# Retention followed by an ELU feed-forward layer: two-level Strassen products replaced by three products of 12-bit float32 parts

## The chip, the cores and the metric

The kernel runs on one core of a Trainium2 chip. The core has a matrix engine (PE; its weight loads are listed apart as PEld), three engines for elementwise work (DVE, ACT, POOL), and a queue (SP) that issues every data transfer (DMA) of this kernel. The metric is the time of one execution in microseconds (us); the median of several executions is given. All times below come from the three timed runs and from one profiled execution of the kernel before.

## The reference

Three steps are computed in float32: a recurrent attention (retention) over 4 batches of 8 heads, 768 tokens and 64 dimensions; then a feed-forward layer from 512 to 2048 features with an ELU; then one from 2048 back to 512.

```python
for t in range(S):                                   # S = 768, H = 8, D = 64
    state = gamma[None, :, None, None] * state + np.einsum('bhd,bhe->bhde', k[:, :, t], v[:, :, t])
    y[:, :, t] = scale * np.einsum('bhd,bhde->bhe', q[:, :, t], state)
x = np.ascontiguousarray(attn_out.transpose(0, 2, 1, 3)).reshape(B * S, H * D)   # 3072 x 512
h = x @ w_in                                         # 512 -> 2048
g = np.where(h > 0.0, h, alpha * (np.exp(np.minimum(h, 0.0)) - 1.0))
return (g @ w_out).astype(np.float32)                # 2048 -> 512
```

## The kernel before

**Blocks.** The 3072 tokens are cut into six blocks of 512. Each block needs its retention first (`scores`, `states`, `outputs`: many float32 products of 64x64), then layer 1 (`w_in`, 16 groups of 128 features, 4 products of 128x128 weights by 512 tokens each) and layer 2 (`w_out`, 4 output groups, 16 products each). Written plainly, one layer of one block is 64 products of a 128x128 weight tile by 512 tokens.

**Opening.** Weights arrive as 64-bit numbers. SP loads sixteen pieces of 1 MB (L149), ACT turns each into float32 parts in three passes (`prepare`, L171, L173, L175), and DVE joins them (`decode`, L198 and L201). Beside that, PE computes the retention of block 0 and its layer 1 by plain float32 products (`plain_first`, L518 and L542), and the scores and states of block 1.

**Strassen.** Everything after that is Strassen's scheme in Winograd's form, which needs 7 half-size products for 8. Layer 2 of block 0 (`second_of_first`, L632) and layer 1 of block 1 (`first`, L765) use one level. Layer 2 of block 1 (`second_twice`, L924) uses two levels. Blocks 2 and 3, and then 4 and 5, are taken together, 1024 tokens at a time: layer 1 uses two levels for four of the seven products (`big_twice`, L1152) and one level for the other three (`big_rest`, L1199), and layer 2 uses two levels throughout (`second_big`, L1248). DVE makes the sums and differences of operands (L894, L1230) and of products (L1260, L1208), ACT moves products out of PE's accumulators (L1163, L1256) and computes the two steps of the ELU (L1214, L1215), which DVE ends (L1216).

**Weights.** Sums of weight blocks are formed once on DVE, written to a scratch area in memory, and read back for every later block in pieces of 128x512 numbers, 256 KB each (`want`, `fetch`, L830), in a fixed order, into a ring of buffers; a buffer is asked for again when PE has done with it.

**Order.** The scheduling is manual: each engine executes its instructions in the order in which the program text issues them. Lists such as `ORDER1`, `BIG2` and `VISITS` say where the retention of the next block goes between the products. POOL has little to do: it multiplies the values of a 128-token chunk by their powers of gamma (`scale_v`, L293), 16 times.

Of the kernel before, what the change touches and what calls it, by code (L numbers as in the profile page):

```python
# [10 lines left out]
FP32 = mybir.dt.float32  # L11
I32 = mybir.dt.int32
# [3 lines left out]
ALU = mybir.AluOpType  # L16


@with_exitstack
def kernel(  # L20
# [4 lines left out]
    scratch: bass.AP,  # L25
    scratch2: bass.AP,
    scratch3: bass.AP,
    scratch4: bass.AP,
# [3 lines left out]

# [6 lines left out]
    C = P  # L60
# [7 lines left out]
    NQ = 4  # L68
    NF = DFF // P // 2
# [7 lines left out]
    epool = ctx.enter_context(tc.tile_pool(name="epool", bufs=2))  # L77
    mid = ctx.enter_context(ExitStack())
    mpool = mid.enter_context(tc.tile_pool(name="mpool", bufs=4))
    hpool = mid.enter_context(tc.tile_pool(name="hpool", bufs=4))  # L80
    small = mid.enter_context(tc.tile_pool(name="small", bufs=6))
# [3 lines left out]

    early = ctx.enter_context(ExitStack())
    stage = early.enter_context(tc.tile_pool(name="stage", bufs=3, side="right"))
    t4 = early.enter_context(tc.tile_pool(name="t4", bufs=1, side="right"))
    so_ = t4.tile([P, 2, 7, 256], FP32, name="so")


    gnames = ["C11", "C12", "C21", "C22", "T3"]
    gq = {x: const.tile([P, DFF // P // 2, TH], FP32, name="g" + x) for x in gnames}
    gq["T1"] = gq["C12"]
    four = lambda x: gq[x].rearrange("p (i a) t -> p i (a t)", a=2)
    g_plain = [four(x)[:, i, :] for x in gnames[:4] for i in range(4)]

# [4 lines left out]
    def load(m, cuts=(0, 2048), behind=None):  # L102

        if m >= NCHUNK:
            return
        t = ldpool.tile([P, 2048], FP32, name="chunk", tag="chunk")
        raw[m] = (
            t[:, 0:1024].rearrange("p (a h c) -> p a h c", a=2, c=C),
            t[:, 1024:2048].rearrange("p (a h d) -> p a h d", a=2, d=D),
        )  # L110
        hold(t, behind)
        for lo, hi in itertools.pairwise(cuts):
            nc.sync.dma_start(t[:, lo:hi], qkv[m, :, lo:hi])

    def hold(t, other):

        if other is not None:
            nc.gpsimd.tensor_copy(t[0:1, 0:1], other[0:1, 0:1])

    w_all = const.tile([P, NQ, 14 * TH], FP32, name="w_all")
    w_a_, w_b_, w_x_ = (
        w_all[:, :, 1024 * g : 1024 * g + 1024].rearrange("p n (f c k d) -> p n f c k d", f=2, c=2, k=2) for g in range(3)
    )
    w_y_ = w_all[:, :, 3072:3584].rearrange("p n (f k d) -> p n f k d", f=2, k=2)
    w_a, w_b, w_x, w_y = ([x[:, n] for n in range(NQ)] for x in (w_a_, w_b_, w_x_, w_y_))
    s_of = lambda n: (w_y[n], w_x[n][:, :, 0], w_x[n][:, :, 1])
    NPIECE = 2 * NQ + NF  # L130
# [20 lines left out]

    def prepare(parts=1, by_vector=False, between=None):

# [4 lines left out]
        if n < 2 * NQ:  # L160
            dst = (w_a, w_b)[n % 2][n // 2].rearrange("p a b c d -> p (a b c d)")
        else:

            dst = w_x[n % NQ].rearrange("p a b c d -> p (a b c d)")
        todo = []
        for part in range(parts):
# [3 lines left out]
            lo, hi, flat = t[:, c, 0], t[:, c, 1], dst.bitcast(U32)[:, c]  # L170
            nc.scalar.activation(flat, lo, AF.Copy, scale=2.0**-29)  # L171
            top = dst.bitcast(F8).rearrange("p (c b) -> p c b", b=4)[:, c, 3]
            nc.scalar.activation(top, hi.bitcast(FP32), AF.Copy, scale=2.0**-120, saturate=False)  # L173
            if not by_vector:
                nc.scalar.activation(lo.bitcast(FP32), hi.bitcast(FP32), AF.Copy, scale=2.0**-112)  # L175
            todo.append((lo, flat, hi if by_vector else None))
        prepared.append((dst, todo))


    ORDER_F = [f for n in range(NF // 2) for f in (n, NF // 2 + n)]  # L180


    quarters = lambda f: scratch.rearrange("(s k) p (f c) -> k f p s c", k=2, f=4)[f // 4, f % 4]

    used = lambda f, a, b: slice(a, b, 2 if f < NF // 2 else 1)

    def decode(fine=False):

# [4 lines left out]
        decoded.append(dst.rearrange("p (a b) -> p a b", a=2))  # L193
        vec = nc.vector
        for c, flat, hi in todo:
            if hi is not None:
                vec.tensor_scalar(c.bitcast(FP32), hi.bitcast(FP32), 2.0**-112, None, ALU.mult)
# [3 lines left out]
            vec.tensor_tensor(out=flat, in0=c, in1=flat, op=ALU.add)  # L201
            yield
        load_piece()
        if n >= 2 * NQ:
            f = ORDER_F[n - 2 * NQ]
            nc.sync.dma_start(quarters(f)[:, used(f, 2, 8)], dst.rearrange("p (s c) -> p s c", c=P)[:, used(f, 2, 8)])
# [4 lines left out]

    blank = hpool.tile([P, TB], FP32, name="blank", tag="h")
    nc.vector.memset(blank, 0.0)

# [9 lines left out]
    begin = so_.rearrange("p n s c -> p (n s c)")  # L226
# [10 lines left out]
    nc.vector.tensor_scalar(vf, vf, scale, None, ALU.mult)  # L237

    causal = begin[:, 2 * S : 2 * S + P]
# [4 lines left out]
    identity = begin[:, 2 * S + P : 2 * S + 2 * P]  # L244
# [9 lines left out]
    post = begin[:, S : 2 * S]  # L254
# [20 lines left out]


    xb = const.tile([P, 4, TB], FP32, name="xb")
    xt_ = const.tile([P, 4, 2, TH], FP32, name="xt")
    xt = [xt_[:, n] for n in range(4)]

    x_of = lambda tb: xb if tb in (0, 3, 5) else xt_.rearrange("p j a t -> p j (a t)")

    xt1 = [xb[:, n].rearrange("p (a t) -> p a t", a=2) for n in (1, 2, 3, 0)]
# [15 lines left out]
    def state(tb, n):  # L299
# [3 lines left out]
        if (tb, n) == (0, 3):  # L303

            return xt[0].rearrange("p a t -> p (a t)")[:, 0:256].rearrange("p (h e) -> p h e", e=D)
# [79 lines left out]
    def outputs(tb, pp):  # L385
# [18 lines left out]
        for sub in range(2):  # L404
            nc.vector.tensor_tensor(
                out=place_of(x_of(tb)[:, :, 2 * pp * C : 2 * (pp + 1) * C])[:, :, :, sub, :], in0=y[sub],
# [67 lines left out]
    def combine_x_parts(tb=None):  # L474
        sub = lambda o, x, y: nc.vector.tensor_tensor(out=o, in0=x, in1=y, op=ALU.subtract)
        b11, b12, b21, b22 = (x_of(tb)[:, 2 * r : 2 * r + 2, half[t]] for r in range(2) for t in range(2))
        t1, t2, t3, t4_ = xt1 if tb == 1 else xt
        sub(t1, b12, b11)
        yield
        sub(t2, b22, t1)  # L480
        yield
        sub(t3, b22, b12)
        yield
        sub(t4_, b21, t2)

# [7 lines left out]
    def elu(g, h, depth=1, then=None):  # L493


        r = epool.tile([P, 512], FP32, name="r", tag="r", bufs=3)
        e = r if len(h.shape) == 2 else r.rearrange("p (a c) -> p a c", c=P)
        nc.scalar.activation(e, h, AF.Relu, scale=-1.0)
        nc.scalar.activation(e, e, AF.Exp, scale=-1.0)

        def last():
            nc.vector.scalar_tensor_tensor(g, e, -1.0, h, ALU.add, ALU.max)
            if then:
                then()

        while len(later) >= depth:
            later.pop(0)()
        later.append(last)

    def plain_first():  # L510

        tiles = [(n, w, row, fi) for n in range(NQ) for w, row in ((w_a, 0), (w_b, 1)) for fi in range(2)]
        banks = []

        def part(k, columns):
            n, w, row, fi = tiles[k]
            for j in range(4):
                nc.tensor.matmul(  # L518
                    banks[k][:, columns], lhsT=w[n][:, fi, j // 2, j % 2, :], rhs=xb[:, j, columns],
                    start=(j == 0), stop=(j == 3), skip_group_check=True,  # L520
                )

        for k in range(5):
            hp = bank("aabd"[k]) if k < 4 else ps_r.tile([P, 2, TH], FP32, name="hp", tag="r")
            banks.append(hp.rearrange("p a b -> p (a b)"))
# [8 lines left out]
        for k in range(5):  # L534
            part(k, half[1])
            n, w, row, fi = tiles[k]
            elu(g_plain[row * NF + 2 * n + fi], banks[k])
            yield
        for k, (n, w, row, fi) in enumerate(tiles[5:]):
            hp = bank("aabd"[k % 4]).rearrange("p a b -> p (a b)")  # L540
            for j in range(4):
                nc.tensor.matmul(  # L542
                    hp, lhsT=w[n][:, fi, j // 2, j % 2, :], rhs=xb[:, j, :], start=(j == 0), stop=(j == 3)
                )
            elu(g_plain[row * NF + 2 * n + fi], hp)
# [3 lines left out]
    def of_first(r, f, t, count=2):  # L549

        i = (r * NF + f) % 4
        g = gq[gnames[(r * NF + f) // 4]]
        return g[:, 2 * i + t] if count == 1 else g[:, 2 * i + t : 2 * i + 4 : 2, :]

    inputs = {}

    def inputs_of_first(f, slots):

        b11, b12, b21, b22 = (of_first(r, f, t) for r in range(2) for t in range(2))
        t3, t2, t4_ = slots  # L560
        tt = lambda o, x, y: nc.vector.tensor_tensor(out=o, in0=x, in1=y, op=ALU.subtract)
        tt(t3, b22, b12)
        tt(b12, b12, b11)
        yield
        tt(t2, b22, b12)
        tt(t4_, b21, t2)
        for x in range(2):
            inputs[f + x] = {
                1: of_first(0, f + x, 0, 1), 2: of_first(1, f + x, 0, 1), 3: of_first(1, f + x, 1, 1),
                4: t4_[:, x], 5: of_first(0, f + x, 1, 1), 6: t2[:, x], 7: t3[:, x],  # L570
            }
        yield

    sums = {}

    def sums_of_pieces(n):

        odd = n // 2 % 2
        t = so_[:, :, 3:7] if odd else so_[:, :, 0:4]
        both = w_all[:, n % NQ : n % NQ + 2, 2048:3072]  # L580
        a21, a11, a12, a22 = (both[:, :, 256 * d : 256 * d + 256] for d in range(4))
# [1307 lines left out]
```

## Time and profile before

| what | value |
|---|---|
| median of 3 runs | 621.36 us (620.31 to 621.38) |
| span of the profiled execution | 621.4 us |
| PE busy | 611.4 us (98%), 5446 records |
| DVE busy | 496.7 us (80%), 776 instructions |
| ACT busy | 261.0 us (42%) |
| POOL busy | 21.2 us (3%) |
| moved by DMA | 125.14 MB, mean 201 GB/s |
| granted clock of PE | 1.00 in every stretch |

The profiled execution's span is within 0.1 us of the median, so its rows can be added up against the measured time directly. A float32 product appears as two matmul records, each with its own weight load. "Mean ns of one" is how long one instruction takes from start to end; matmuls follow each other faster than that, since the next starts while the one before drains, so the pace of PE has to be read from runs of many records.

### The profile page before, as it was taken

The page shows a single profiled execution, that of the slowest core. Times are in us where ns is not written, and L with a number is a line of the kernel's source. Part 1 is how long each engine was busy: PE and PEld are TensorE (multiplying, and loading weights), DVE is VectorE, ACT ScalarE, POOL GpSimd, SP SyncE. Part 2 cuts the span into 40 slices and gives each one's busy share as a digit, 9 for nine tenths or more (in the row PEclk, how much of TensorE's full clock was granted, in tenths as well). Part 3 has the DMA queues.
Part 4 walks back from the last instruction along what each step waited for, and adds up shares of the span by engine and source line. Part 5 has one row for each costly group of instructions (what it writes and reads, how often), then busy time and mean ns, then how long its engine had stood idle before and what let it go on. Part 6 is the DMA issues. An engine that isn't in the chain of part 4 may idle for free.

```text
span 621.4 us, 13415 instructions
## 1 busy us (share of the span) xinstructions
PE 611.4 (98%) x5446; PEld 480.9 (77%) x5446; DVE 496.7 (80%) x776; ACT 261.0 (42%) x446; POOL 21.2 (3%) x30
## 2 busy tenths in 40 slices
PE   8999999999999999999999999999999999999998
PEld 6764568888889998888545888888888744788886
DVE  5768889989889875677888987898546897888885
ACT  5888844205542111236898210100144798511110
POOL 2011000000000001000010000110000000000000
PEclk9999999999999999999999999999999999999999
DMA  8697569789575898786811445873654523356453
GB/s 295 285 374 303 174 205 269 235 242 274 204 234 151 301 374 310 231 250 199 274 49 67 122 134 154 268 275 108 206 159 143 151 69 93 118 148 187 153 150 117
DMA packets 79278, 125.14 MB, mean 201 GB/s; under 512 B 6128, under 2 KB 46832, under 8 KB 74480
## 3 DMA queue, kind: packets, MB, share of 16 engines
q1 hardware_dynamic: 79216, 124.28, 62.1%
q8 instruction: 43, 0.70, 0.4%
q14 instruction: 19, 0.16, 0.1%
HBM read 94.63 MB, written 29.62 MB: 200 GB/s over the span
## 4 chain that ended last, share of the span: by engine, by line
PE 86%; DVE 4%; DMA 3%; ACT 3%; issue 2%; SPq 0%; DVEq 0%
PE pa L1248 15%; PE pa L1152 9%; PE pd L1248 8%; PE pa L1199 6%; PE pd L1152 4%; PE pa L765 4%; PE pd L1199 4%; PE pb L1248 4%; PE x L632 3%; DMA wq<-scratch_dram 2%; PE pa L924 2%; PE pa L542 2%; PE pb L1152 2%; PE pa L632 2%; PE pb L1199 2%; PE y L415 2%
## 5 line engine op out<-in xcount | busy, mean ns | idle before, releaser
L1256 ACT COPY ms<-pa 128x256 f32<-128x256 f32 x41 | 15.3, 372 | 108.5 <-PE pa L1248 105.5
L1248 PE MATMUL pa<-gC,wq 128*128 128x256 f32 x224 | 53.1, 381 | 0.0
L1248 PEld LDWEIGHTS pa<-gC,wq 128*128 128x128 f32 x224 | 42.1, 190 | 6.8 <-DVE gT L1216 0.5
L1215 ACT ACTIVATE r<-r 128x512 f32<-128x512 f32 x64 | 40.3, 630 | 2.0
L1163 ACT COPY m<-pa 128x512 f32<-128x512 f32 x32 | 18.7, 585 | 48.9 <-PE pa L1152 48.8
L293 POOL TENSOR_TENSOR chunk<-chunk,vf 128x512 f32<-128x512 f32 x16 | 18.0, 1124 | 381.3 <-DMA chunk<-in_qkv_dram 201.1
L1260 DVE TENSOR_TENSOR res<-pd,ms 128x256 f32<-128x256 f32 x26 | 11.0, 422 | 25.0 <-PE pd L1248 14.1
L1152 PE MATMUL pa<-ts,wq 128*128 128x256 f32 x104 | 26.9, 384 | 0.0
L1248 PE MATMUL pa<-ts,wq 128*128 128x256 f32 x112 | 26.8, 382 | 0.0
L1248 PE MATMUL pd<-w_all,wq 128*128 128x256 f32 x112 | 26.6, 380 | 0.1
L171 ACT ACTIVATE w_all<-wraw 128x1024 uint32<-128x1024 uint32 (+1 forms) x19 | 19.2, 1008 | 16.9 <-PE x L632 9.0
L1248 PE MATMUL pd<-ts,wq 128*128 128x256 f32 x104 | 24.7, 380 | 0.2 <-DVE ts L894 0.2
L1230 DVE TENSOR_TENSOR gC<-w_all,gC 128x1024 f32<-128x1024 f32 x20 | 24.2, 1260 | 0.0
L1248 PEld LDWEIGHTS pd<-w_all,wq 128*128 128x128 f32 x112 | 21.2, 190 | 3.4 <-DVE w_all L894 0.6
L1248 PEld LDWEIGHTS pa<-ts,wq 128*128 128x128 f32 x112 | 21.0, 190 | 2.9
L1248 PE MATMUL pa<-w_all,wq 128*128 128x256 f32 x96 | 22.9, 381 | 0.0
L173 ACT ACTIVATE w_all<-wraw 128x1024 fp8e4<-128x1024 f32 (+1 forms) x19 | 22.6, 1189 | 0.6
L1152 PEld LDWEIGHTS pa<-ts,wq 128*128 128x128 f32 x104 | 19.3, 190 | 4.5 <-ACT m L1163 0.8
L1216 DVE SCALAR_TENSOR_TENSOR w_all<-r,w_all 128x512 f32<-128x512 f32 x32 | 22.0, 688 | 0.7 <-ACT r L1215 0.6
L1248 PEld LDWEIGHTS pd<-ts,wq 128*128 128x128 f32 x104 | 19.7, 190 | 3.2 <-DVE ts L894 0.6
L1199 PE MATMUL pa<-ts,wq 128*128 128x512 f32 x48 | 22.1, 592 | 0.0
L1199 PE MATMUL pa<-gC,w_all 128*128 128x512 f32 x48 | 22.1, 592 | 0.0
(327 smaller groups left out, 1458.0 us busy)
## 6 DMA issues: line engine op xcount, KB each, us to landing
wq<-scratch_dram SPq DMA_DIRECT2D x191, 256.0 KB, 3.2
chunk<-in_qkv_dram SPq DMA_DIRECT2D x22, 1024.0 KB, 7.6
wraw<-in_w_dram SPq DMA_DIRECT2D x15, 1024.0 KB, 7.1
out_dram<-res SPq DMA_DIRECT2D x7, 512.0 KB, 3.3
scratch_dram<-gT SPq DMA_DIRECT2D x12, 256.0 KB, 4.3
wq<-scratch_dram SPq DMA_DIRECT2D x24, 128.0 KB, 3.1
scratch_dram<-w_all SPq DMA_DIRECT2D x12, 256.0 KB, 3.4
scratch_dram<-w_all SPq DMA_DIRECT2D x24, 128.0 KB, 3.2
```

The source lines that it names most:

```text
L171: nc.scalar.activation(flat, lo, AF.Copy, scale=2.0**-29)
L173: nc.scalar.activation(top, hi.bitcast(FP32), AF.Copy, scale=2.0**-120, saturate=False)
L293: eng.tensor_tensor(out=v, in0=v, in1=vf[:, i].unsqueeze(2).to_broadcast([C, H, D]), op=ALU.mult)
L632: nc.tensor.matmul(X[j][:, d, :], lhsT=w[j][:, d * P : d * P + P], rhs=x[j], start=(n == 0 and d == 0), stop=at_end, skip_group_check=True,)
L765: nc.tensor.matmul(ps[:, fi, :], lhsT=w[:, fi, j2, :], rhs=x[:, j2, :], start=(begin and fi == 0 and j2 == 0), stop=(j2 == 1), skip_group_ ...
L1152: nc.tensor.matmul(ps[:, f, :], lhsT=w[:, f, :], rhs=big_xs[j][k], start=(begin and f == 0), stop=True, skip_group_check=True,)
L1163: nc.scalar.copy(o, ps)
L1199: nc.tensor.matmul(ps, lhsT=w[:, k, :], rhs=layer_x[j][:, k], start=False, stop=(k == 1), skip_group_check=True,)
L1215: nc.scalar.activation(r, r, AF.Exp, scale=-1.0)
L1216: return lambda: nc.vector.scalar_tensor_tensor(g, r, -1.0, g, ALU.add, ALU.max)
L1230: nc.vector.tensor_tensor(out=quarter(to, r, t), in0=quarter(x, r, t), in1=quarter(y, r, t), op=op)
L1248: nc.tensor.matmul(ps, lhsT=w[:, f, :], rhs=ts[j][k][:, f // 2, f % 2, :], start=(begin and f == 0), stop=(f == 3), skip_group_check=True,)
```

## The change

All Strassen code goes, together with its sums, its four scratch areas and its ring (some 1,000 lines). Layer 1 of block 0 stays as it was. Every other layer becomes three products of parts, in the type float32r:

- Each operand is cut into a high part of 12 bits (`hi`), the rest (`lo`), and a third part `d` that is made from the two. The product is the sum of `hi` by `hi` and `lo` by `lo`, scaled in the accumulator by 1 + 2^-12 (`scaled`), plus the product of the two `d`.
- Weights of layer 1 are cut in block 1 (`parts_of_w_in`: one instruction on ACT, one on DVE, two transfers of 256 KB to scratch); `d` of them is made by POOL, for every 128 features in every block (`third_of_w_in`). Weights of layer 2 are cut in block 0 (`parts_of_w_out`: one on ACT, two on DVE over 128x1024, two transfers of 512 KB). From block 2 on, each 128x512 part is read back from scratch: `hi` and `lo` of `w_in`, `lo` and `d` of `w_out`; `hi` of `w_out` stays in place.
- Activations are cut in every block: `split_g` per 128 features (ACT, DVE, and DVE again, or POOL in block 0), and `split_x` (two halves: ACT, DVE, DVE).
- Each of the five blocks 1 to 5 is now computed alone, layer 1 and then layer 2. Retention of the next block goes between groups of layer 1 (`visit`, at groups 4, 6, 8, 10, 12).

Lines that begin with + in the core of the diff:

```diff
+    def parts_of_w_out(m):
+        src, hi = decoded[NPW + m], flat(wo1[:, 2 * m : 2 * m + 2])
+        lo = wpool.tile([P, 1024], F32R, name="p2", tag="p2", bufs=3)
+        d = wpool.tile([P, 1024], F32R, name="p3", tag="p3", bufs=1)
+        nc.scalar.activation(hi, src, AF.Copy, scale=PART * CUT)
+        stt(lo, src, PART, hi, ALU.subtract)
+        stt(d, hi, R, lo, ALU.subtract)
...
+    def split_g(f, by_pool=False):
...
+        nc.scalar.activation(g_hi[f], g[f], AF.Copy, scale=R * CUT)
+        stt(g_lo[f], g_hi[f], -1.0 / R, g[f], ALU.add)
+        (nc.gpsimd if by_pool else nc.vector).tensor_tensor(out=g_d[f], in0=g_lo[f], in1=g_hi[f], op=ALU.subtract)
...
+    def third_of_w_in(tb, f):
+        if f < NF:
+            got[tb, 4, f] = ring.tile([P, TB], F32R, name="w3", tag="w3", bufs=3)
+            nc.gpsimd.tensor_tensor(out=got[tb, 4, f], in0=got[tb, 1, f], in1=got[tb, 0, f], op=ALU.subtract)
...
+    def one_pass(ps, w, x, start=False, stop=False):
+        nc.tensor.matmul(ps, lhsT=w, rhs=x, start=start, stop=stop, skip_group_check=True)
...
+    def first(tb, f):
+        hp = flat(ps_r.tile([P, 2, TH], FP32, name="hp", tag="r") if f < 2 else bank("aabd"[(f - 2) % 4]))
+        for n in range(2):
+            for k in range(NK):
+                one_pass(hp, got[tb, n, f][:, k * P : k * P + P], xp[:, n, k], start=(n == 0 and k == 0))
+        scaled(hp, tb == 1 and f % 2 == 1)
+        yield
+        for k in range(NK):
+            one_pass(hp, got[tb, 4, f][:, k * P : k * P + P], xp[:, 2, k], stop=(k == NK - 1))
+        elu(f, hp)
...
+    def second_layer(tb, acc, between=None, beside=lambda f: None):
+        for f in range(3):
+            second(tb, acc, f, (0, 1))
+        if between:
+            between()
+            flush()
+        for f in range(NF):
+            second(tb, acc, f, (2, 3) if f < 3 else range(4))
+            if tb:
+                fetch()
+            if f + 3 < NF:
+                split_g(f + 3, tb == 0)
+            beside(f)
...
+    second_layer(0, acc, None, beside_first)
+    mid.close()
+    ring = ctx.enter_context(tc.tile_pool(name="ring", bufs=8))
+    want_out(0)
+    fetch(8)
```

In layer 2, `second` issues the first two products of a group for its output groups, and `end_of_second` issues the third products of all 16 groups after the accumulators have been scaled. In block 0, `beside_first` puts `parts_of_w_out` and the decoding of the next weight piece beside groups 1, 3, 5, 7 and 9 of layer 2; the other three pieces are cut during layer 1 of block 0.

## The prediction

> **What bounds the kernel now.** I read the busy shares first, then the chain that ended last, then the chain in order of time, and then single groups by shape.
>
> ```profile
> PE 611.4 (98%) x5446; PEld 480.9 (77%) x5446; DVE 496.7 (80%) x776; ACT 261.0 (42%) x446; POOL 21.2 (3%) x30
> ...
> PE 86%; DVE 4%; DMA 3%; ACT 3%; issue 2%; SPq 0%; DVEq 0%
> ```
>
> PE works nearly without a break and carries 86% of the chain. DVE is 80% busy, but its work lies beside PE's. So a change pays by the PE time it removes, less the waits of PE that it adds. The pace of PE stands in the chain in order of time:
>
> ```profile
> 86.57 2.59 PE x L632 x12
> ...
> 297.49 1.72 PE pa L1199 x4
> ...
> 348.67 2.02 PE sc L319 x128
> ...
> 362.97 2.01 PE kv L359 x110
> 364.99 1.93 PE pa L1248 x8
> 366.91 1.73 PE pb L1248 x8
> ```
>
> Eight records of 256 columns take 1.73 us, 0.216 each; four of 512 take 1.72, 0.430 each. A float32 product has two records, so 128x128 by 512 columns costs 0.860. The reader should also see that each record loads its own weights (190 ns a load in the groups list) and that this load hides wholly behind 0.216 of matmul. After retention (L319, L359) the next eight records take 1.93, that is, 0.2 more. The opening, plain float32, lasts until 86.4 us, where L632 begins.
>
> **The change, part by part.**
>
> *Removed.* From 86.4 us on: L632 and L765 (224 records each), L1152 (448), L1248 (784) at 0.216; L1199 (192) at 0.430; L924 (392 of 128 columns, sixteen in 1.79 us, so 0.112). That is 1680 x 0.216 + 192 x 0.430 + 392 x 0.112 = 489 us of PE, and all Strassen sums of DVE.
>
> *Added on PE.* 192 products of parts in layer 2 of block 0, and 384 in each of five blocks: 2112, each one pass of 512 columns with one weight load. No float32r product is in this trace. A part of 12 bits is half of a float32 number's 24, so a product of parts should need one of the four products of halves that make up a whole one: a quarter of 0.860, 0.215. The nearest row is the 256-column record: it loads 128x128 weights of 4 bytes as well and costs 0.216. The ends are 0.112 (the 128-column record) and 0.430 (the 512-column record). I take 0.216: 2112 x 0.216 = 456 us. The saving in streaming is thus only 33 us: two levels of Strassen over four such passes cost 49/64 x 4 = 3.06, and here there are 3; most of the 33 comes from layers that had one level.
>
> *Kept.* The opening, 86.4 us. Outputs of block 1 and the retention of blocks 2 to 5: scores 2.02, states 2.01, outputs about 3.8 a block, so 4 x 7.8 + 3.8 = 35, and 0.2 for some 20 returns from it: 39 us. Without any wait of PE: 86.4 + 456 + 39 = 581.6 us. Before, the same count is 86.4 + 489 + 39 = 614, so its waits and end are 7 us. The question is whether the new waits stay under 39.8 us.
>
> *Waits, A: groups 1 to 10 of layer 2 of block 0.* There a weight piece is decoded and another cut for every two groups. DVE: two `g_lo` (0.69 each, L1216's row), two 128x1024 subtractions (1.22, L894 and L1230), decoding 0.69 and 1.29: 5.8 us. ACT: 1.16 + 1.37 + 1.15 for the piece, about 1.1 for `hi` and 2 x 0.63 for `g_hi`: 6.0. PE: 16 x 0.216 = 3.5. In addition POOL makes two `g_d`, and POOL and DVE get in each other's way:
>
> ```profile
> 45.22 1.17 POOL L293 TENSOR_TENSOR chunk<-chunk,vf 128x512 f32<-128x512 f32 x1 [3.92 <-DMA chunk<-in_qkv_dram]
> ```
> ```profile
> 45.40 1.53 DVE L561 TENSOR_TENSOR h<-gC,gC 128x512 f32<-128x512 f32 x1
> 46.97 0.69 DVE L561 TENSOR_TENSOR gC<-gC 128x512 f32<-128x512 f32 x1
> ```
>
> The same subtraction takes 1.53 beside POOL's multiplication and 0.69 alone; L1208, which reads one operand from the accumulators, keeps 0.69 beside POOL (at 308.75). `g_lo` and the two cuts read two operands from SBUF, so POOL's 2 x 1.04 adds to DVE's 5.8: 7.9 us a pair, 4.4 more than PE. Five pairs: 22 us. If the two ran side by side it would be 2.5 x 5 = 12.
>
> *B: start of the third products of block 0.* The ring lies where the buffers of the cuts were (`mid.close()`), so its first transfer waits for the last PE read of those and lands 3.2 us later (row `wq<-scratch_dram`); POOL's last `g_d` are late as well, about 2. I take 5 us; nothing covers it.
>
> *C: borders.* Where layer 1 ends, the last group goes PE, ACT (0.59), ACT (0.63), DVE (0.69) before its accumulator is free for layer 2: 2.1 us against some 0.3 of other work, so 1.8. The first three groups of layer 2 each wait for `g_hi` and `g_lo` (0.63 + 0.69 against four products, 0.86): about 1.5 together. In layer 1, banks and buffers come late after the five visits of retention: 2 to 3. Some 6 us a block, 30 for five. Within the groups nothing binds: per group of layer 1 PE takes 2.59 and ACT 1.81 (two of 0.59, one of 0.63); per group of layer 2 PE 1.73 and DVE 1.38. In block 1 ACT has 2.1, DVE 1.7, POOL 1.04 a group: hidden too, but with 0.5 to spare.
>
> *D: end.* Last copy 0.59 and store: 3.5 us.
>
> *DMA.* SP's queue carries weights all the time: 64 transfers of 256 KB, 4 chunks of 1 MB and the outputs, 22 MB a block. The queue moved 124.28 MB in 62.1% of 621.4 us, so 322 GB/s when busy: 0.81 us per 256 KB. Third products need one per 0.86 us, and layer 2's first part 16 x 0.81 + 4 x 3.3 = 26 us in 27.6. I count it as hidden; the cover is thin.
>
> Sum: 581.6 + 22 + 5 + 30 + 3.5 = **642 us**, 3.3% slower than 621.4. The gain of 33 us on PE is there, and 57 us of waits for DVE, ACT, POOL and transfers come in its place, against 7 in the kernel before.
>
> **One rule weighed.** The rows above show 0.216 us per 512 column-passes, never less, over 784 records of L1248. The Trainium skill, page "TensorE: Matmul & The Clock Gate", section "Back-to-back issue gap", gives for a stream of weight loads and matmuls of 512 columns about 131 ns each, and calls the 216 ns of the single gap too high. By that figure the passes would take 2112 x 0.131 = 277 us (an estimate from that page). No row here comes near it. Another page of the Trainium skill, "FP8 and Floating Point Precision", section "TensorE Precision Notes", says that true float32 makes four passes; 0.860 against 0.215 would fit it; the trace has no single pass.
>
> **The rivals.**
>
> 1. *The engines keep up: faster.* DVE and POOL do not exclude each other in block 0, and the borders are covered by the first groups' products. A falls to 12, C to 10, B stays: 581.6 + 12 + 5 + 10 + 3.5 = 612. It decides as soon as all waits are under 39.8 us. For it: ACT and DVE are under PE's time in every steady group. Against it: the row of 1.53, and that the border is a chain of one engine after the other. Chance 0.11.
> 2. *A pass of float32r streams as long as a record of 512 columns does, 0.430.* Then 2112 x 0.214 is added, and PE's slack covers waits: about 1070 us. Against it: one product of halves is a quarter of the work, not half. No row excludes it. Chance 0.08.
> 3. *POOL or the transfers are heavier than here.* POOL's subtraction writes float32r, which no row shows; at 2 us instead of 1.04, A grows by 5 x 2 x 1, block 1 (where a group has 2.6 us) by some 9, and borders by 8: about 670. Or DMA at 322 GB/s or less binds in layer 2 and the third products: 2 to 4 us a block, 655 to 660. Chance 0.17 for 655 to 690.
> 4. *A pass takes 0.112 to 0.131.* Then DVE, ACT and DMA set the pace (per block ACT 16 x 1.81 + 8 = 37 in layer 1, then DVE 16 x 1.38 = 22, then DMA 16 x 0.81 = 13: 72 us; block 0 some 70): 86 + 70 + 5 x 72 + 4, with some waits about 530. No record of 512 columns in the trace is under 0.430. The Trainium skill's 131 ns ("TensorE: Matmul & The Clock Gate") would fall here too. Chance 0.02.
> 5. *No change:* waits of 39 to 41 us, between the forecast and rival 1. Chance 0.02.
>
> **How the numbers follow.** Forecast (634 to 655): 0.60. Runs of this kernel can tell 0.2% from no change, so faster is below 620.1 (rivals 1 and 4, 0.13), the same up to 622.6 (0.02), slower the rest (0.85). The range 612 to 668 holds the forecast, no change, about half of rival 1 and most of rival 3: 0.60 + 0.02 + 0.05 + 0.13 = 0.80; rivals 2 and 4 lie outside.
>
> **What would show it.** In the profile after: eight L539 records in 1.73 us (rivals 2 and 4 show 3.4 or 1.0); PE's busy share down to about 90%; layer 2 of block 0 with PE idle for DVE in the slices from 86 to 140 us, and `g_lo` (L494) and the cuts (L175, L176) over 1.4 us beside POOL's L495; a gap of some 3 us at the first third product; gaps of about 2 us at each border of layers, ended by DVE. Five equal blocks of about 97 us would confirm C; longer ones, with DMA as the releaser, would be rival 3. Wrong I would be, above all, if the pass is not 0.216.

## The result and the profile after

The changed kernel takes 674.68 us (median of 4 runs, 672.59 to 678.55) against 621.36: a ratio of 1.0866 (95% interval 1.0826 to 1.0906). It is slower, as forecast, but 33 us slower than the 642 of the forecast and 7 us beyond the end of the range. The profiled execution took 676.4 us, 1.7 more than the median; its rows cover 674.6 us from the first instruction to the last, and below they are added up to that. (Wherever both are on record, for the kernel before too, a span is some 2 us shorter than the time of the same execution, so span and median can be compared only that closely.)

The page of the changed kernel, first the busy shares and the chain that ended last:

```profile
PE 630.6 (93%) x5294; PEld 484.9 (72%) x5294; DVE 363.1 (54%) x543; ACT 316.8 (47%) x486; POOL 157.1 (23%) x130
...
PE 81%; ACT 7%; DVE 5%; DMA 4%; issue 2%; SPq 0%; DVEq 0%; ACTq 0%
```

PE was to be busy for some 580 us and is busy for 631. Its share fell only to 93%, and it still carries 81% of the chain: the miss is not mainly waiting, PE itself is busy for longer than I counted. The slices of the same page, in tenths of the span's fortieth parts, show where the rest is:

```profile
PE   7998977787999899999899999899999899999897
...
PEclk9999779888999999999999999999999999999999
```

A slice is 16.9 us. PE is less than full in slices 6 to 10, which is layer 2 of block 0, and the granted clock falls under full there and just ahead of it; in the kernel before it was full everywhere. After that come five equal blocks.

The pace of a pass is read from stretches between the starts of two passes. In the changed kernel, twelve passes of layer 1 of block 2 and twelve of its third products (columns: busy time and number of records of each engine, granted clock, DMA share; the two or so extra records overlap an edge of the stretch):

```profile
288.68:291.48 2.80, 2.80 (x14) 2.26 (x13) 0.88 (x2) 1.63 (x3) 0.98 (x1) 1.00 0.52 151
362.08:364.80 2.72, 2.72 (x14) 2.25 (x13) 2.69 (x3) 0.00 (x0) 0.00 (x0) 1.00 0.72 228
```

At full clock a pass takes 2.80 / 12 = 0.233 us in layer 1 and 2.72 / 12 = 0.227 in layer 2, not 0.216. With the starts of the stages from the trace, each term of the forecast gets its measured size:

| term | forecast | measured | how |
|---|---|---|---|
| opening | 86.4 | 86.9 | first pass of layer 2 of block 0 |
| 2112 passes | 456 | 485 | 1152 x 0.2267 + 960 x 0.2333 |
| kept retention | 39 | 37 | 4 x 8.2, and 4.3 in block 0 |
| A, layer 2 of block 0 | 22 | 22.6 | 58.3 from its start to its end, less 128 x 0.2267, less 4.3 of retention, less 2.4 that belong to B |
| B, third products of block 0 | 5 | 12.8 | 24.9 less 64 x 0.2267, and 2.4 ahead of them |
| C, borders | 30 | 26 | per block 102.1 less 88.3 of passes, less 8.2: 5.6; 5.1 and 4.3 in the first and last |
| D, end | 3.5 | 4.0 | |
| sum | 642 | 675 | |

The opening is one of the parts that differ from execution to execution: in the six profiled ones that have the same code up to there it ended between 82.1 and 86.9 us, so differences of 1 or 2 us in a total are read from the stages and not from the total. The granted clock goes along with it. Where the opening shows no stretch at half the clock (border, below) it ended at 82.1 us; with one stretch of 3.4 us (align, late_prep, align96) at 84.3 to 85.8; with 6.8 us (late_load, and the changed kernel itself) at 86.5 and 86.9. Which of the two causes the other is not shown. But the 86.9 of the table meets the forecast's 86.4 by luck: at full clock the new opening is some 4 us shorter than the old one.

The kernel before was timed again beside each experiment and took 621.8 to 623.1 us (median). So a gain read from the ratios comes out up to 3 us larger than one read from the times; where it matters, the stages decide.

So 29 of the 33 us are one term, the pace; 8 are B, and C gives 4 back; the other terms differ by 2 us or less. Three things had to be found out: why a pass takes 0.227, and 0.233 in layer 1; what B consists of; and whether A and C have the causes that I gave them. The half clock is inside A, B and the opening.

### The profile page after: what moved, and what is told of

Its sections match the earlier page's. It is cut to its first block, busy times and chain, and to the rows that moved or that the text cites. A ratio compares the mean times of both kernels' runs of the same rounds, so it can differ in the third digit from the quotient of the medians.

```text
span 674.6 us, 13408 instructions
## 1 busy us (share of the span) xinstructions
PE 630.6 (93%) x5294; PEld 484.9 (72%) x5294; DVE 363.1 (54%) x543; ACT 316.8 (47%) x486; POOL 157.1 (23%) x130
## 4 chain that ended last, share of the span: by engine, by line
PE 81%; ACT 7%; DVE 5%; DMA 4%; issue 2%; SPq 0%; DVEq 0%; ACTq 0%
PE pa L539 36%; PE pd L539 15%; PE pb L539 15%; PE hp L539 4%; PE kv L322 2%; PE pa L462 2%; ACT r L449 2%; PE y L378 2%; PE y L393 2%; DVE p L166 1%; DMA wraw<-in_w_dram 1%; DVE gl L166 1%; PE sc L282 1%; DMA w<-scratch_out_dram 1%; DMA chunk<-in_qkv_dram 1%
## 5 line engine op out<-in xcount | busy, mean ns | idle before, releaser
L536 POOL TENSOR_TENSOR w<-w 128x512 fp32r<-128x512 f32 x80 | 103.2, 1290 | 273.0 <-PE pd L539 68.0
L539 PE MATMUL pa<-xp,w 128*128 128x512 f32 x480 | 123.7, 398 | 0.0
L539 PEld LDWEIGHTS pa<-xp,w 128*128 128x128 f32 x480 | 88.9, 188 | 23.9 <-DMA w<-scratch_in_dram 2.3
L493 ACT ACTIVATE gh<-g 128x512 fp32r<-128x512 f32 x96 | 59.6, 629 | 78.8 <-PE pa L539 67.5
L166 DVE SCALAR_TENSOR_TENSOR gl<-gh,g 128x512 fp32r<-128x512 f32 x96 | 70.5, 738 | 38.2 <-ACT gh L493 37.5
L539 PE MATMUL pa<-gh,wo 128*128 128x512 f32 x192 | 77.6, 404 | 8.0 <-DVE g L453 8.0
L539 PE MATMUL pa<-gl,w 128*128 128x512 f32 x160 | 62.4, 390 | 0.0
L450 ACT ACTIVATE r<-r 128x512 f32<-128x512 f32 x96 | 60.6, 631 | 3.1
L495 DVE TENSOR_TENSOR gd<-gl,gh 128x512 fp32r<-128x512 f32 x80 | 59.1, 739 | 2.7
L453 DVE SCALAR_TENSOR_TENSOR g<-r,pa 128x512 f32<-128x512 f32 x48 | 32.8, 683 | 48.7 <-ACT r L450 48.7
L539 PE MATMUL pa<-gd,w 128*128 128x512 f32 x192 | 56.9, 405 | 0.1
L539 PEld LDWEIGHTS pa<-gh,wo 128*128 128x128 f32 x192 | 37.3, 194 | 17.8 <-DVE g L453 10.2
L539 PE MATMUL pd<-gh,wo 128*128 128x512 f32 x96 | 39.8, 415 | 9.2 <-ACT gh L493 5.3
L539 PE MATMUL pd<-xp,w 128*128 128x512 f32 x180 | 48.1, 402 | 0.0
L539 PE MATMUL pb<-xp,w 128*128 128x512 f32 x180 | 46.9, 395 | 0.0
L539 PEld LDWEIGHTS pa<-gd,w 128*128 128x128 f32 x192 | 37.8, 197 | 8.3 <-DVE pa L543 0.4
L539 PE MATMUL pd<-gd,w 128*128 128x512 f32 x96 | 36.5, 406 | 7.0 <-DMA w<-scratch_out_dram 4.8
L495 POOL TENSOR_TENSOR gd<-gl,gh 128x512 fp32r<-128x512 f32 x16 | 27.7, 1745 | 59.3 <-DVE gl L166 55.7
L539 PEld LDWEIGHTS pb<-xp,w 128*128 128x128 f32 x180 | 33.8, 188 | 8.2
```

Source lines behind the costliest of these rows:

```text
L166: (eng or nc.vector).scalar_tensor_tensor(o, a, by, b, ALU.mult, op)
L453: later.append(lambda: nc.vector.scalar_tensor_tensor(g[f], e, -1.0, h, ALU.add, ALU.max))
L493: nc.scalar.activation(g_hi[f], g[f], AF.Copy, scale=R * CUT)
L495: (nc.gpsimd if by_pool else nc.vector).tensor_tensor(out=g_d[f], in0=g_lo[f], in1=g_hi[f], op=ALU.subtract)
L536: nc.gpsimd.tensor_tensor(out=got[tb, 4, f], in0=got[tb, 1, f], in1=got[tb, 0, f], op=ALU.subtract)
L539: nc.tensor.matmul(ps, lhsT=w, rhs=x, start=start, stop=stop, skip_group_check=True)
```

## The experiments

### What a pass costs

**m1, m2 and m3** are streams of products with all else left out, so that only pace is measured. The core of m1:

```python
def mm(b, wt, xt):
    nc.tensor.matmul(b, lhsT=wt, rhs=xt, start=True, stop=True, skip_group_check=True)
for n in range(48):
    mm(bk[n % 4], W(w, n), X(x, n, 512))      # and other operands, widths, banks, types
```

> Streams of 48 matrix products by themselves, everything else of the computation left out (the output holds the last stream's sums). Theory T: a float32r product of 512 columns takes 0.227 us of its own, in one bank or rotating banks, with rotating or fixed weights, and the streams beside transfers, ACT, DVE and POOL keep 0.227; a float32 record of 256 columns takes 0.216, a bf16 product 0.216. The 0.233 of layer 1 should come back in one of the streams that read a moving operand laid out like xp or that sum in one bank. Rival R1 (contention): 0.216 alone, 0.227 to 0.233 only beside transfers or beside another engine's work. Rival R2 (bound by the weight load): 0.227 stays at 384 and 256 columns; under T 384 columns take some 0.17.

The stretches of m1, from the first to the last start of 48 products (47 intervals): float32r of 512, 384 and 256 columns, bf16 of 512, float32r with the moving operand laid out like `xp` and summed in one bank, and float32r beside DVE:

```profile
22.03:32.69 10.66, 10.66 (x49) 8.82 (x47) 0.00 (x0) 0.00 (x0) 0.00 (x0) 1.00 0.01 2
54.67:62.84 8.17, 8.17 (x48) 8.16 (x47) 0.00 (x0) 0.00 (x0) 0.00 (x0) 1.00 0.01 2
63.02:68.64 5.62, 5.62 (x48) 5.62 (x48) 0.00 (x0) 0.00 (x0) 0.00 (x0) 1.00 0.00 0
105.09:115.23 10.14, 10.14 (x48) 4.57 (x47) 0.00 (x0) 0.00 (x0) 0.00 (x0) 1.00 0.01 2
142.81:153.79 10.98, 10.98 (x48) 8.82 (x47) 0.00 (x0) 0.00 (x0) 0.00 (x0) 1.00 0.00 0
186.71:197.36 10.65, 10.65 (x49) 8.82 (x47) 8.32 (x13) 1.97 (x4) 0.00 (x0) 1.00 0.01 2
```

That is 0.2268, 0.1738, 0.1196, 0.2157, 0.2336 and 0.2266 us a product. Nothing contends: alone, in one bank or four, with fixed or rotating weights, beside transfers (195 GB/s), ACT, DVE or POOL it is 0.227 each time. 128 columns fewer take 53 to 54 ns less, and bf16, which takes 0.1091 at 256 columns, comes to the same pace (53.3 ns for 128 columns). What is left beside the streaming is some 13 ns for float32r and 2.4 for bf16. R1 (contention) and R2 (the weight load) fall, T stands: 0.227 is the type's own. What in the engine takes the 11 ns more, the runs do not tell. A float32 record of 256 columns took 0.216 here too, so the row that I took the price from was measured rightly; it was another type's row. The Trainium skill, page "TensorE: Matmul & The Clock Gate", section "Wait — 56ns, not 53.3ns?", gives 215.7 ns from start to start for 512 columns; the bf16 stream agrees with 215.7, the float32r stream (226.8) does not.

The place of `xp` alone brought 0.233. In m1 that operand began 32 bytes past a multiple of 64, and I took that for the cause.

> Streams of 48 products again, everything else left out. In the first set only the operand that lay at the top of SBUF, at an address of 32 modulo 64 bytes (as xp does in the changed kernel), took 0.233 in place of 0.227. Theory T2: it is the alignment: at the top of SBUF but at a multiple of 64 bytes 0.227; at the bottom at 32 modulo 64 bytes 0.233, with 384 columns also some 6 ns more than 0.173; weights at 32 modulo 64 bytes and bf16 or float32 operands at 32 are open, I expect no more than some ns. Rival: it is the place at the top of SBUF: 0.233 there though aligned, 0.227 at the bottom though not.

The alignment theory fell. At the top of SBUF and aligned: 0.227; at the bottom, not aligned: 0.233, as expected. But the operand that had taken 0.227 in m1, aligned and at the same address, now took 0.233: only the weights lay elsewhere. With 384 columns there was no difference (0.173). What was common to all the fast streams was the distance of the two operands, a multiple of 512 bytes.

> Streams of 40 float32r products of 512 columns, everything else left out. The 0.227 and 0.233 of the two sets so far do not follow the alignment of one operand: the same moving operand took 0.227 with weights that lay a multiple of 512 bytes from it and 0.233 with others. Theory T3: what counts is the distance of the two operands' addresses, modulo 512 bytes or a part of it: with both at the same place, or both shifted by the same 32, 64 or 128 bytes, 0.227; with the moving operand 32, 64, 96, 128 ... 224 bytes off, 0.229 to 0.234; again 0.227 at 256 or at 512 bytes off. Rival: the absolute place of one operand counts; then shifting both also gives 0.233. A bf16 stream with 96 bytes between them keeps 0.216.

| moving operand's address less the weights', bytes | 0 | 32 | 64 | 96 | 128 | 160 | 192 | 224 | 256 | 384 | 512 | 640 | 768 |
|---|---|---|---|---|---|---|---|---|---|---|---|---|---|
| ns a product | 226.7 | 233.3 | 229.0 | 233.4 | 233.3 | 234.4 | 233.3 | 233.2 | 227.2 | 233.2 | 226.9 | 233.2 | 226.9 |

Three of these streams as the trace shows them (40 products each; distance 0, distance 32, both operands shifted by 32):

```profile
18.38:27.44 9.06, 9.06 (x41) 7.51 (x40) 0.00 (x0) 0.00 (x0) 0.00 (x0) 1.00 0.01 2
27.45:36.78 9.33, 9.33 (x41) 7.50 (x40) 0.00 (x0) 0.00 (x0) 0.00 (x0) 1.00 0.00 0
147.66:156.74 9.08, 9.08 (x41) 7.51 (x40) 0.00 (x0) 0.00 (x0) 0.00 (x0) 1.00 0.00 0
```

T3 holds, with a period of 256 bytes in these steps of 32: only the distance counts, shifting both changes nothing (227.3 to 227.7), and a distance of -192 gives the 229 of 64. A bf16 stream at 96 bytes keeps 215.8. What in PE or SBUF makes it so, these runs do not tell.

**align and align96** carry this into the kernel. `xp` lay 96 bytes (modulo 256) from the ring; a pad above it moves it to 64 and to 0.

```diff
-            xp = ctx.enter_context(tc.tile_pool(name="xp", bufs=1, side="right")).tile([P, 3, NK, TB], F32R, name="xp")
+            right = ctx.enter_context(tc.tile_pool(name="xp", bufs=1, side="right"))
+            xp = right.tile([P, 3, NK, TB], F32R, name="xp")
+            right.tile([P, 8], FP32, name="pad")        # align96: [P, 24]
```

> A pad of 32 bytes above xp, which puts xp at a multiple of 64 bytes; nothing else changes. Theory T2 (alignment of the moving operand): the 960 products of layer 1 go from 0.233 to 0.227, each block's layer 1 from 53.5 to 52.3 us, the whole to 668 to 670. Rival (place at the top, or POOL's and the transfers' traffic in layer 1): no change, 673 to 676.

> xp is moved down by 96 bytes, so that it lies a multiple of 512 bytes from the weights' ring (with 32 bytes the passes of layer 1 took 0.229). Theory T3 (distance of the operands): layer 1's passes take 0.227 as in layer 2, 960 x 6 ns = 6 us less than the changed kernel: 667 to 670. Rival: layer 1 keeps 0.229 to 0.233 for another reason: 671 to 675.

align: 671.08 us (ratio to before 1.0786, 1.0739 to 1.0832), layer 1's passes at 0.229. It missed its 668 to 670, since the alignment that it was built on was the wrong rule; 0.229 is what the table has for 64. align96: 669.83 us (1.0776, 1.0745 to 1.0807), layer 1 at the pace of layer 2:

```profile
288.52:291.24 2.72, 2.72 (x14) 2.25 (x13) 0.89 (x2) 1.59 (x3) 0.94 (x1) 1.00 0.60 178
```

So 6 ns x 960 of the miss are where a buffer happened to lie, and most of them come back by moving it 96 bytes: 4.8 us by the medians, 3.9 in the five blocks of the two profiled executions.

### A: layer 2 of block 0

**plain_b0** computes this layer as plain float32 products, straight from the decoded pieces (four buffers for these, one for `p2`), and leaves the cuts of `w_out` beside it. The third products go, and with them the weights that they fetched; the loads of block 2's chunks, the cut of `x` and one step of retention now lie beside the plain products, so A and B are both taken away.

```diff
-    second_layer(0, acc, None, beside_first)
+    plain_second(acc, beside_first)     # one_pass(acc[d], decoded[NPW + f // 2][...], g[f]) for all f and d
...
-    want_out(0)
-    fetch(8)
...
+    parts_of_w_in(0)
+    parts_of_w_in(1)
```

> Layer 2 of block 0 as plain float32 products (64 of 0.860, 55 us), straight from the decoded weights; the cuts of w_out remain beside it, g_hi, g_lo and g_d of block 0 fall away, and so do its third products. Theory T: PE then waits for nobody there (per two groups PE 6.9, DVE 4.5, ACT 5), the clock stays full, and 58.3 + 24.9 = 83.2 us become 55 + some 4 (retention outputs) + 3 (first cut of w_in): 62; the whole 652 to 658. Rival (waits only move to the next place, ring and weights late in block 1): 662 to 672.

653.38 us (1.0535, 1.0464 to 1.0607). From 84.0 to 144.6 us, where the changed kernel needs 83 us, it needs 60.6, and PE is busy for nearly all of it:

```profile
84.00:144.60 60.60, 59.99 (x369) 27.87 (x367) 33.82 (x38) 24.19 (x25) 0.00 (x0) 1.00 0.59 215
```

Four passes for each product, 55 us, are faster here than three passes, 43.5, with 35 us of waits A and B. The rival (waits that only move) falls: block 1 takes 101.7 us, against 101.6.

**gd_dve and late_prep** ask what A consists of. The first gives POOL's subtractions to DVE, the second takes ACT's work on the next piece out of the way of `g_hi`.

```diff
-            split_g(n - 13, True)
+            split_g(n - 13)
...
-                split_g(f + 3, tb == 0)
+                split_g(f + 3)
```

```diff
             parts_of_w_out(f // 2 + 3)
-            next_piece()
+            decode_all()
+        elif 2 <= f < 8:
+            prepare()
```

> The 16 subtractions g_d of block 0 on DVE in place of POOL. Theory T (POOL and DVE exclude each other on two SBUF operands): the cuts of w_out go from 1.82 and 2.03 back to some 1.22 us (12 of them, -8.5 us), g_lo from 0.77 to 0.69 (-1), DVE gets 16 x 0.69 = 11 us more: the first part of layer 2 of block 0 stays within 3 us of 58.3, the whole within 671 to 678. Rival: the long cuts come from the float32r output and not from POOL: they stay long and DVE's 11 us come on top, 682 to 687.

> In layer 2 of block 0 ACT's three passes over the next weight piece are issued one group later, behind the next g_hi, in place of right behind the cut whose DVE half must first free the buffer. Theory A1 (as forecast: DVE's and POOL's work a pair, some 8 us, sets the pace): no change, 58 us for the first part, 673 to 677 in all. Rival A2: the pace is set by the order of ACT's queue (cut by ACT, cut by DVE, then the piece's three passes, and only then g_hi): the first part falls by 4 to 8 us, 666 to 671.

The DVE groups of this stretch by shape, in the changed kernel and then in gd_dve (the first two rows below are the two subtractions of a cut, which read two operands from SBUF):

```profile
L166 DVE SCALAR_TENSOR_TENSOR p<-wo,p 128x1024 fp32r<-128x1024 f32 x6 | 12.2, 2033 | 0.2
...
L166 DVE SCALAR_TENSOR_TENSOR p<-wtmp,wo 128x1024 fp32r<-128x1024 f32 x6 | 10.9, 1818 | 1.3 <-ACT wo L174 1.3
```

```profile
L166 DVE SCALAR_TENSOR_TENSOR p<-wo,p 128x1024 fp32r<-128x1024 f32 x5 | 6.1, 1225 | 0.2
L166 DVE SCALAR_TENSOR_TENSOR p<-wtmp,wo 128x1024 fp32r<-128x1024 f32 x5 | 6.1, 1218 | 0.0
```

POOL's `g_d` of the changed kernel in the same stretch, and the same kind of subtraction alone in m1, with float32 and with float32r output:

```profile
L495 POOL TENSOR_TENSOR gd<-gl,gh 128x512 fp32r<-128x512 f32 x16 | 27.7, 1745 | 59.3 <-DVE gl L166 55.7 <-DVE seen L362 3.6
```

```profile
L110 POOL TENSOR_TENSOR pol<-raw 128x512 f32<-128x512 f32 x11 | 14.1, 1283 | 202.3 <-DVE pol L108 201.5
L117 POOL TENSOR_TENSOR pr<-x 128x512 fp32r<-128x512 f32 x9 | 11.4, 1268 | 0.6
```

Beside POOL a cut's subtraction takes 1.8 to 2.0 us, without POOL 1.22, so the rival (the float32r output makes the cuts long) falls; POOL's subtraction gets longer too, 1.75 for 1.27 alone. Row by row against gd_dve, DVE's work is some 10 us longer beside POOL, as the forecast had it (5 x 2.08). Moving POOL's work to DVE gives the same total, 672.72 us (1.0777 to 1.0839), and 57.7 us for the stretch: whichever engine does it, the sum of the two is what counts. late_prep changed nothing either, 675.76 us (1.0837 to 1.091) and 59.2 us: it is not the order of ACT's queue. So DVE with POOL's share sets the pace of A in the main. Not alone: DVE works 47.9 of the 58.3 us and spends most of the other 10 waiting for ACT's `g_hi` (4.2) and for retention on PE (4.4), and no run takes these waits away by themselves.

### B: the third products of block 0

In the changed kernel, while these 64 products run, PE works 19.9 of 25 us and the DMA engines are 0.94 busy (second row; the first is the stretch of A):

```profile
86.70:145.00 58.30, 43.80 (x370) 31.90 (x368) 47.89 (x48) 30.75 (x38) 27.65 (x16) 0.85 0.46 169
145.00:170.00 25.00, 19.92 (x64) 14.70 (x65) 8.22 (x10) 4.44 (x6) 2.55 (x2) 0.80 0.94 347
```

PE's waits there are for the weights; the second one, ahead of the first third product, has no releaser in the profile:

```profile
PE pd L539 <- DMA w<-scratch_out_dram: 4.8, 3, 2.7
PE pd L539 <- issue: 2.2, 1, 2.2
```

The largest entries of the list of transfers for the same 25 us name what fills them; a write to scratch lands after 10.6 us here, where the median of the whole execution is 2.1:

```profile
chunk<-in_qkv_dram SPq DMA_DIRECT2D x4, 1024.0 KB, 9.9
w<-scratch_out_dram SPq DMA_DIRECT2D x10, 256.0 KB, 4.5
scratch_in_dram<-w SPq DMA_DIRECT2D x4, 256.0 KB, 10.6
```

**late_load** takes only the four chunks away from there:

```diff
-        if n in (1, 3, 5, 7):
-            load(2 * CPB + n // 2)
...
+            if f in (0, 1, 2, 3) and tb == 1:
+                load(2 * CPB + f)          # scale_v and visit of block 1 follow 2 to 4 groups later
```

> The four chunks of 1 MB for block 2 are loaded in layer 1 of block 1 and no longer beside the third products of block 0; the retention of block 2 moves back by two to four groups. In the changed kernel these products got 16 weight transfers of 256 KB and the chunks, 8.4 MB in 24.9 us, with the DMA engines 0.87 to 1.02 busy. Theory B1 (the transfers set the pace there, and the opening of the ring only the first 3 us): third products 17 to 20 us in place of 24.9, nothing lost in block 1, 667 to 671. Rival B2 (the ring's late opening and the late g_d set it, as forecast): 23 to 25 us and 673 to 677. Rival B3 (the loads are only moved): block 1 gets longer by what block 0 gains, 673 to 677.

668.57 us (1.0734, 1.0697 to 1.0772), and the third products take 16.6 us in place of 24.9:

```profile
144.70:161.30 16.60, 16.36 (x64) 12.85 (x65) 8.17 (x10) 4.44 (x6) 2.58 (x2) 0.90 0.85 299
```

B1 holds, with a stage even shorter than the 17 to 20 us expected. The waits for the weights are gone, and 6 passes run at half the clock in place of 15. So 8.3 of B's 12.8 us come from transfers that I had counted as hidden, some 2 of them through slow passes that follow the waits. The opening of the ring, which I had given 5, costs the 2.4 ahead of the first product and little more; the first weight was asked for at 142.0 us, 3.2 before that product, which fits, but no run moves the ring alone. Block 1 does not get longer (101.7 us, against 101.6).

### The clock

In the changed kernel 25 passes of A and 15 of B follow each other at 0.427 us, at half the clock, after PE has waited. At 0.2 us each that is 8 us, and I suspected that all of it counted.

**clk and clk2** put products of zeros, which add nothing to the sums, where PE waits: clk in A and B, clk2 in B alone.

```diff
+    def idle_passes(acc, count):
+        for _ in range(count):
+            one_pass(acc[0], zero[:, 0:P], zero)        # bf16 zeros
...
+            idle_passes(acc, 6)                         # ahead of the third products; 4 each ahead of groups 8 to 11
...
+            if not tb and 0 < f < 12:                   # clk alone
+                idle_passes(acc, 5)
```

> Block 0's layer 2 with 77 bf16 products of zeros (0.216 each, 16.6 us) put into PE's queue ahead of the products that waited longest; they add zero to an accumulator. Theory T: PE's idle stretches let the granted clock fall to one half, which cost some 8 us; the products fit into the waits (17 us and 8 us), the clock stays 1.0 after 86 us, the result is 666 to 670. Rival: the half clock has another cause (the start of float32r work, power): it stays and the time is the same or up to 5 us longer, 674 to 680.

> 22 of the zero products alone, those ahead of the third products of block 0 (none in the first part of its layer 2). Theory T: the half clock costs time only where PE sets the pace, so in the third products, and nothing in the first part where PE waits anyway: third products 20 to 21 us in place of 24.9, the first part 58 as in the changed kernel, the whole 670 to 673 (of the gain 1 to 2 us may go to a wait for the first cuts of block 1). Rival: the half clock costs nothing anywhere, since transfers bound the third products: 24 to 25 us and 674 to 677.

clk took 677.58 us (1.0899, 1.085 to 1.0949), not 666 to 670:

```profile
83.10:145.10 62.00, 53.38 (x431) 35.20 (x429) 49.25 (x52) 31.88 (x40) 26.60 (x16) 0.92 0.44 161
145.10:165.40 20.30, 18.63 (x80) 13.05 (x81) 6.84 (x8) 3.29 (x5) 2.55 (x2) 1.00 1.00 365
```

In B the zero products keep the clock full, and it falls to 20.3 us. In A the clock is still at half for 22 passes, and A rises to 62.0; probably not all of the 55 products there fell into waits. clk2 took 673.11 us (1.0819, 1.0792 to 1.0846):

```profile
84.80:142.50 57.70, 42.75 (x376) 30.34 (x374) 48.80 (x49) 30.71 (x38) 27.61 (x16) 0.91 0.46 170
142.50:164.00 21.50, 19.15 (x80) 13.03 (x81) 8.18 (x10) 4.41 (x6) 2.55 (x2) 1.00 0.98 357
```

B gains 3.4 us (21.5 in place of 24.9, where 20 to 21 were expected), A stays (57.7), and block 1 is 2 us longer, of which 1.2 are a wait for a cut of `w_in`. In A only 9 passes happened to be slow here, in place of 25, and it is hardly shorter: where DVE sets the pace, a slow PE costs next to nothing. So the half clock of these two stages costs 1 to 3 us, not 8; the total, 1.6 us less, is not clear of noise, and the figure rests on the stages. clk2 and late_load both shorten B, so their gains do not add: with late_load B is already within 2.1 us of its 64 passes.

### C: the borders, and all together

**border** moves the last two visits of retention to the border of the layers, where they use up waits:

```diff
-            if f in (4, 6, 8, 10, 12):
+            if f in (4, 6, 8):
                 visit(tb + 1, f // 2 - 2)
...
+        visit(tb + 1, 3)
         second_layer(tb, acc, lambda: run(before), beside)
...
             flush()
+            visit(tb + 1, 4)
```

> The last two visits of retention (some 1.9 and 1.4 us of PE) are moved from the middle of layer 1 to the border of layers 1 and 2, where PE waits some 1.8 us for the last banks of layer 1 and g_hi, and 1.8 us for the last g, in blocks 1 to 4. Theory T (borders are a chain PE, ACT, DVE that other PE work can cover): 2.5 to 3.2 us less a block, 662 to 666. Rival (retention's own operations of DVE go ahead of g and g_lo in DVE's queue and keep the banks longer): less than 4 us gained in all, 670 to 677.

664.35 us (1.0653, 1.0606 to 1.0699). PE's waits of block 2, first in the changed kernel and then in border (L453 is the last step of the ELU; `gl` is `g_lo`):

```profile
PE pa L539 <- DVE g L453: 1.6, 1, 1.6
PE pd L539 <- DVE g L453: 0.7, 1, 0.7
PE pb L539 <- DVE gl L166: 0.2, 1, 0.2
```

```profile
PE pa L539 <- DVE g L453: 0.3, 1, 0.3
PE pb L539 <- DVE gl L166: 0.2, 1, 0.2
```

The border was the chain PE, ACT, DVE that the forecast described, and other PE work covers it: 2 us in the waits listed, and 2.4 to 2.9 in each of the blocks 1 to 4.

**best1** joins plain_b0, align and border.

> Plain float32 layer 2 in block 0, xp aligned, and the two visits at the border, together. If the three gains are independent (21 from the plain layer, 5 to 6 from alignment, 10 to 13 from the borders): 634 to 639. If the alignment or the border gives nothing, 640 to 650. Faster than the kernel before (621 to 623) under no theory: 5 x 384 x 0.2265 = 435 us of passes + 86 + 55 + 39 is 615 before any wait.

640.72 us (1.0284, 1.0244 to 1.0324). That is just above the 634 to 639 expected, in the range named for one gain missing. None is missing, but alignment (by 32 bytes, as in align) brought less than the 5 to 6 us put in: alone, the three had gained 21.3, 3.6 and 10.3 us on the 674.7, and together 34.0, so they are nearly independent. No version here beats the kernel before. The count leaves little room for it: 435 us of passes for five blocks (at 0.2267), 55 for block 0, the opening and the retention are 615 without any wait, 6 us under the kernel before, and best1 lies 26 above that.

## Why the prediction missed

- **The failed step** is the price of a pass: "I take 0.216: 2112 x 0.216 = 456 us". The passes take 485. Of the 29 us, 2112 x 0.0107 = 23 are the type's own cost, which the record of another type could not show (m1), and 960 x 0.0066 = 6 are the place of `xp` (m3, align96). I had bounded the price by 0.112 and 0.430 and then treated the middle as known. The range of -30 and +26 us allowed the pass only 12 ns up if all else was right; a step of 5% in a term that makes up seven tenths of the total is 23 us.
- With it falls "The saving in streaming is thus only 33 us". Removed are 489 us, added 485: 4. The change had nothing to pay its waits with.
- **B** was mis-sized, 12.8 for 5. Rival 3's second half (the transfers bind) was right in this one place, at 347 GB/s: not by the weights alone, as I had it, but with the four chunks among them in SP's queue. "The cover is thin" was written, and not followed to the stretch where the loads lie.
- **A** was right in size (22.6 for 22) and in the main cause, DVE and POOL in each other's way (gd_dve, late_prep). The close agreement is partly luck. `g_lo` was to exceed 1.4 us and stayed at 0.77 in the mean, so most of the loss fell on the cuts; POOL's subtraction takes 1.27 alone, not the 1.04 that I took from its multiplication; and DVE's waits for ACT and PE were not in the sum. Rival 1 needed A at 12 and C at 10 and did not come about.
- **C** was right in cause, and 26 for 30. In block 2 PE loses 4.0 us at the border, where I had 1.8 and 1.5, and 1.0 in layer 1, where I had 2 to 3; two wrong sizes nearly cancel. Blocks took 102 us, not 97, which is 5.4 us more for their 384 passes, not longer borders. D and the retention held within 2 us, the opening by luck. Unforeseen was the half clock, 1 to 3 us in A and B.
- Rivals 2 and 4 fell with the pace of L539: no pass at 0.430 at full clock, and no product of 512 columns near 0.131 in m1. POOL's subtraction to float32r took 1.29 in the mean in layer 1 (L536) and 1.75 beside DVE in block 0 (L495), under the 2 of rival 3; the output's type makes no difference in m1.

## What to carry to other kernels

A price that no row shows and that is multiplied by thousands decides the forecast: carry its error into the range in per cent of that term, and do not count a row of another type as its price. An exchange of PE schemes that saves a few per cent of streaming must be weighed against the work that its operands need where PE has no slack to wait: here, in block 0, plain four-pass products beat three passes that waited for their operands. Follow every load that shares a queue into the stretch where it will run, and ask of a slow clock or a wait first whether that engine sets the pace there.

## What the runs showed of the hardware

- A float32r product of 128x128 by 512 columns takes 0.2266 us, bf16 0.2157, a float32 one 0.860 in the kernel before; the 11 ns that float32r has more than bf16 at 512 columns are as many at 256 (0.1196, bf16 0.1091).
- At 512 columns it takes 229 to 234 ns when the addresses of its two operands differ by other than a multiple of 256 bytes (steps of 32 were tried), in a stream by itself (m3) as in the kernel (0.233, and 0.227 after a move of 96 bytes). At 384 columns (0.173), and with bf16 at 96 bytes (0.2158), no such difference was seen.
- The granted clock fell to one half for stretches of 3.4 or 6.8 us after PE had waited, and passes then took 0.427. The Trainium skill, page "TensorE: Matmul & The Clock Gate", section "What's actually happening", speaks of an activity window of 3.4 us and of half the clock after an idle one. The lengths here agree, one or two such windows; but PE's idle times ahead of these stretches in layer 2 of block 0, or as they began, were 1.5 to 3.6 us, mostly shorter than a window, and one of 2.7 us (from 103.8) was followed by none.
- A DVE subtraction of 128x1024 from two SBUF operands took 1.22 us alone and 1.82 to 2.03 in the mean beside POOL. POOL's subtraction of 128x512 took 1.27 alone (m1) and 1.75 (L495) in that company.
